# First batch of a sorted-block attention and feed-forward kernel: processed in two block halves, with a hand-written order and the second half under the feed-forward

## Chip, cores and metric

The kernel runs on one core of a Trainium2 chip. The metric is the device time of one execution in microseconds (us). Every time of a kernel below is a median; a figure from a trace is that of the one profiled run. Runs of different calls went to different chips, so kernels of different calls are compared by their ratios to the kernel before.

## The reference, cut to what matters

Attention with a learned block sort, then a bilinear feed-forward. There are 4 batches, 8 heads, 768 rows, head size 64, and 8 blocks of 96 rows.

```python
for _ in range(5):                       # per head, an 8 x 8 matrix
    P = exp(P - max(P)); P = P / sum(P, axis=-1); P = P / sum(P, axis=-2)
k_sorted = einsum('bhij,bhjcd->bhicd', P, k_blocks)   # "mix"; v likewise
scores = q_block @ k_sorted_block.T / 8               # each block on its own
x = softmax(scores) @ v_sorted_block
out = ((x @ w_a) * (x @ w_b)) @ w_out                 # 512 -> 1536 -> 512
```

## The kernel before

A unit of attention is a group: two heads of one batch, 768 rows, four groups to a batch. TensorE transposes q (`q_ps`), mixes k and v with the normalised P (`mix`), makes scores (`sc`) in two tiles of four blocks, transposes v (`vs_ps`), multiplies (`o_ps`), and transposes the result back (`xt_ps`). ScalarE copies k and half of v and does the exp. VectorE copies the rest, takes the reciprocal and scales (`xp`). The first batch goes ahead of everything, and each later batch runs as units between the feed-forward steps of the batch before it:

```python
def C0(g):
    stage_mix(g, "k", ps0, "A", ("act",))
    stage_mix(g, "v", ps0, "A", ("act", "dve"))
def R0(g):
    stage_scores(g, ps0, "A")
    stage_v(g, ps0b, "B")
def O0(g):
    stage_o(g, ps0, "A")
for g in range(1, HP):
    stage_q(g, ps0b, "B")
C0(0); C0(1); R0(0); O0(0); to_xT(0, ps0b, "B")
C0(2); R0(1); O0(1); to_xT(1, ps0b, "B")
C0(3); R0(2); O0(2); to_xT(2, ps0b, "B")
R0(3); O0(3); to_xT(3, ps0b, "B")
# ... then, for each batch b:
steps = [lambda m=m, t=t, b=b: ffn_ab(b, m, t, psF) for m in range(KO) for t in range(2)]
# ... after step s, so many of the next batch's 16 units (mix, scores, o, xT of four groups):
want = -(-(s + 1) * len(units) // (n - 2))
```

TensorE's instructions run in the order written: in the timeline the first mix, whose k and P are there by 14.1 us, starts at 17.68 us, behind the transpose of a q that lands at 17.04 us. GpSimd issues all loads but that of the sort matrix in one stream: the first batch's k, v, q group by group, then w_a and w_b, then the second batch's k, v, q. After those come the spreading of P for the later batches (`s_all`), and w_out.

The softmax here doesn't subtract the row's maximum and nothing guards it: scores larger than these inputs give would overflow.

## Time and profile before

| | before |
|---|---|
| time | 276.93 us (276.44 to 277.31, 3 runs) |
| span of the profiled run | 275.0 us |
| first feed-forward matmul | 44.83 us |
| TensorE busy after 44.83 us | nearly without a gap |

These are lines of the page of the kernel before. The PE and PEclk lines cut the span in 40 slices of 6.9 us; a digit is the busy share in tenths, and PEclk is the granted TensorE clock in tenths.

```profile
span 275.0 us, 5700 instructions
...
PE   0267757999999999999999999999999999999993
...
PEclk9998775999999999999999999999999999999999
```

From the eighth slice on TensorE is full. What can be gained quickly lies in the first seven slices, the "head".

The chain of waits of the kernel before, for one group of the head (start, length, what):

```profile
25.50 1.42 PE mix L145 x24
26.92 0.82 PE sc L166 x16
27.74 0.86 PE vs_ps L177 x8
28.62 0.70 DVE vs_116 L179
29.32 0.04 issue
29.36 0.43 PE o_ps L189 x8
29.81 0.21 DVE rec L193
30.05 0.69 DVE xp L196
30.74 0.13 DVE rec L193
30.89 0.70 DVE xp L196
31.59 0.05 issue
31.63 0.45 PE xt_ps L215 x4
32.08 1.42 PE mix L145 x24
```

One group is a chain through three engines, walked in strict order: mixes, scores, v, VectorE's copy, o, two reciprocal and xp pairs, back-transposes, 6.6 us in all. TensorE holds only part of it. The other part shows among its waits up to 46 us:

```profile
engine line waited for: us in total, times, longest us
...
PE xt_ps L215 <- DVE xp L196: 4.7, 8, 0.8
...
PE q_ps L131 <- DMA q_102<-in_q_dram: 2.4, 1, 2.4
PE o_ps L189 <- DVE vs_115 L179: 1.6, 2, 0.8
```

TensorE waits for xp eight times. The fourth q (q_102) lands late and holds back mixes whose own data are ready. The v copy is waited for twice in the buffer shown and once in each of the two others (0.8 us each).

The windows view of the kernel before (stretch in us, then busy time and instruction count of each engine, then the granted clock):

```profile
core 0: us, PE busy (x) PEld busy (x) DVE busy (x) ACT busy (x) POOL busy (x), PEclk, DMA share, GB/s
...
25.00:28.00 3.00, 3.00 (x48) 2.53 (x49) 0.96 (x2) 1.68 (x4) 1.20 (x3) 0.50 1.32 203
...
38.00:44.83 6.83, 4.12 (x52) 3.22 (x53) 3.80 (x8) 1.50 (x2) 6.81 (x5) 0.54 1.07 164
44.83:48.60 3.77, 3.77 (x30) 2.11 (x31) 0.78 (x2) 0.48 (x1) 3.77 (x7) 0.50 0.83 118
```

The granted clock falls to 0.50 in 25 to 28 us, in 32 to 35 us, and from 38.6 us into the feed-forward, until 48.8 us. Two mixes (24 matmuls) take 1.42 us of the chain at a granted clock of 0.50 here, and 0.67 us later in the span.

### The profile page before, as it was taken

The numbers are of one execution on the slowest core, as the hardware profiler recorded it, in microseconds if no ns is written. First come the engines' busy times: TensorE is split into PE (matmuls) and PEld (weight loads), VectorE is DVE, ScalarE is ACT, GpSimd is POOL, SyncE is SP. The second block draws the span as 40 slices with busy tenths as digits, with TensorE's granted clock in tenths as the row PEclk, the third lists the DMA queues.
The fourth block names the chain that finished last, engine by engine and source line by source line (L and its number), as shares of the span: only waits on it lengthen the run. The fifth ranks groups of instructions, "written<-read, shape, count | busy, mean of one in ns | idle before, by whom it ended". The sixth has DMA issues, their size and how long they took to land.

```text
span 275.0 us, 5700 instructions
## 1 busy us (share of the span) xinstructions
PE 247.8 (90%) x2400; PEld 152.7 (56%) x2408; DVE 130.7 (48%) x284; ACT 98.1 (36%) x194; POOL 48.7 (18%) x67
## 2 busy tenths in 40 slices
PE   0267757999999999999999999999999999999993
PEld 0255544766666545666665546666665456656441
DVE  5835553566565413656564415656654214444211
ACT  2024430535446004463635105354552023333100
POOL 8953489446303000000000000000000000000000
PEclk9998775999999999999999999999999999999999
DMA  7999998999844332000000231000001230000132
GB/s 94 183 202 203 203 200 119 182 201 201 129 74 56 70 114 79 0 4 0 2 2 0 79 114 41 1 2 0 2 4 38 79 114 0 0 2 0 38 117 76
DMA packets 22393, 20.82 MB, mean 76 GB/s; under 512 B 1376, under 2 KB 19296, under 8 KB 22368
## 3 DMA queue, kind: packets, MB, share of 16 engines
q0 software_dynamic: 18864, 14.16, 34.4%
q1 hardware_dynamic: 3504, 6.30, 6.1%
q8 instruction: 19, 0.31, 0.5%
q14 instruction: 6, 0.05, 0.0%
HBM read 28.32 MB, written 6.29 MB: 126 GB/s over the span
## 4 chain that ended last, share of the span: by engine, by line
PE 88%; DVE 4%; DMA 3%; POOL 2%; issue 1%; ACT 0%; DVEq 0%
PE pf L231 46%; PE po L247 22%; PE mix L145 5%; PE vs_ps L177 4%; PE sc L166 3%; PE o_ps L189 3%; DMA q_102<-in_q_dram 3%; PE q_ps L131 2%; PE xt_ps L215 2%; DVE xp L196 2%; DMA p_nat<-in_sort_net_dram 1%; DVE vs_115 L179 1%; DVE rec L193 0%; POOL v_88 L78 0%; POOL q_96 L78 0%
## 5 line engine op out<-in xcount | busy, mean ns | idle before, releaser
L240 DVE TENSOR_TENSOR hT<-a_sb,pf 128x384 bf16<-128x384 bf16 x96 | 53.1, 553 | 66.2 <-PE pf L231 55.1
L231 PE MATMUL pf<-xT,w_a_sb 128*128 128x384 bf16 x384 | 78.9, 328 | 0.6 <-DVE xT L217 0.6
L231 PE MATMUL pf<-xT,w_b_sb 128*128 128x384 bf16 x384 | 78.8, 328 | 0.0
L239 ACT CAST a_sb<-pf 128x384 bf16<-128x384 f32 x96 | 46.0, 479 | 76.8 <-PE pf L231 53.0
L247 PE MATMUL po<-w_out_sb,hT 128*128 128x512 bf16 x280 | 62.9, 379 | 0.3
L231 PEld LDWEIGHTS <-w_b_sb 128*128 128x128 bf16 x384 | 37.8, 98 | 25.3 <-issue 0.7
L231 PEld LDWEIGHTS <-w_a_sb 128*128 128x128 bf16 x384 | 35.1, 98 | 21.8 <-issue 1.1
L247 PEld LDWEIGHTS <-hT 128*128 128x128 bf16 x288 | 27.8, 98 | 32.1
L253 DVE COPY o_sb<-po 128x512 f32<-128x512 f32 x12 | 8.3, 692 | 36.6 <-PE po L247 36.6
L251 ACT COPY o_sb<-po 128x512 f32<-128x512 f32 x12 | 7.0, 585 | 50.2 <-PE po L247 34.9
L196 DVE TENSOR_TENSOR xp<-o_ps,rec 96x512 bf16<-96x512 f32 x32 | 21.2, 684 | 0.5
L215 PE MATMUL xt_ps<-ident,xp 96*128 96x96 bf16 x128 | 9.4, 214 | 4.9 <-DVE xp L196 4.7
L217 DVE COPY xT<-xt_ps 128x768 bf16<-128x768 bf16 x16 | 8.9, 554 | 8.9 <-PE xt_ps L215 8.9
L215 PEld LDWEIGHTS <-xp 96*128 96x128 bf16 x128 | 7.3, 101 | 7.7 <-DVE xp L196 5.9
L155 ACT CAST kT_106<-mix 128x384 bf16<-128x384 f32 x12 | 5.2, 482 | 16.6 <-PE mix L145 16.6
L170 ACT ACTIVATE eT_112<-sc 96x768 bf16<-96x768 f32 x12 | 9.0, 802 | 4.6 <-PE sc L166 4.6
L135 DVE COPY qT<-q_ps 128x768 bf16<-128x768 bf16 x16 | 8.7, 551 | 2.7 <-PE q_ps L131 2.7
L193 DVE RECIPROCAL rec<-o_ps 96x8 f32<-96x8 f32 x32 | 5.2, 185 | 8.9 <-PE o_ps L189 8.9
L170 ACT ACTIVATE eT_114<-sc 96x768 bf16<-96x768 f32 x10 | 7.5, 807 | 0.9 <-PE sc L166 0.9
L170 ACT ACTIVATE eT_113<-sc 96x768 bf16<-96x768 f32 x10 | 7.5, 807 | 0.9 <-PE sc L166 0.9
L131 PE MATMUL q_ps<-ident,q_81 128*64 128x128 bf16 x12 | 0.8, 314 | 7.7 <-DMA q_81<-in_q_dram 7.7
L155 ACT CAST kT_108<-mix 128x384 bf16<-128x384 f32 x10 | 4.3, 482 | 7.6 <-PE mix L145 7.6
(208 smaller groups left out, 204.0 us busy)
## 6 DMA issues: line engine op xcount, KB each, us to landing
out_dram<-o_sb SPq DMA_DIRECT2D x24, 256.0 KB, 2.0
w_a_sb<-in_moe_w_a_dram POOLq DMA_DIRECT2D x4, 384.0 KB, 12.8
w_b_sb<-in_moe_w_b_dram POOLq DMA_DIRECT2D x4, 384.0 KB, 13.4
w_out_sb<-in_moe_w_out_dram POOLq DMA_DIRECT2D x3, 512.0 KB, 8.6
k_77<-in_k_dram POOLq DMA_DIRECT2D x1, 192.0 KB, 3.7
v_79<-in_v_dram POOLq DMA_DIRECT2D x1, 192.0 KB, 4.1
q_81<-in_q_dram POOLq DMA_DIRECT2D x1, 192.0 KB, 4.8
k_86<-in_k_dram POOLq DMA_DIRECT2D x1, 192.0 KB, 4.7
```

Of the source, the lines that this page charges most:

```text
L135: nc.vector.tensor_copy(out=qT.rearrange("p i c t -> p c i t"), in_=q_ps.rearrange("p c (i t) -> p c i t", i=NB))
L145: nc.tensor.matmul(mix[e * D:(e + 1) * D, c // 3, c % 3 * P:(c % 3 + 1) * P], lhsT=src2[:, e, c * D:(c + 1) * D], rhs=s_all[:, 2 * g + e], ...
L155: nc.scalar.copy(out=d1, in_=s1)
L170: nc.scalar.activation(out=eT[:, hf, :, 0:HB], in_=sc[0:BLK, :, 0:HB], func=AF.Exp, scale=float(scale))
L177: nc.tensor.matmul(vs_ps[:, i], lhsT=vT[:, i * BLK:i * BLK + P], rhs=ident, is_transpose=True)
L196: nc.vector.tensor_tensor(out=_ap(xp, hf * NBH * 2 * D, [[NB * 2 * D, BLK], [D, 2], [2 * D, NBH], [1, D]]), in0=_ap(o_ps, 0, [[1024, BLK], ...
L215: nc.tensor.matmul(xt_ps[:, i, :], lhsT=xp[:, i], rhs=ident[0:BLK, 0:BLK], is_transpose=True)
L217: nc.vector.tensor_copy(out=xT[:, g % HP, :].rearrange("p (i t) -> p i t", i=NB), in_=xt_ps)
L231: nc.tensor.matmul(pf[:, 0:HW], lhsT=w_sb[:, kc, m * P:(m + 1) * P], rhs=_ap(xT, kc * S + t * 3 * CG, [[KA * S, P], [CG, 3], [BLK, NB], [1 ...
L239: nc.scalar.copy(out=a_sb, in_=pf[:, 0:HW])
L240: nc.vector.tensor_mul(out=hT[:, m, t * HW:(t + 1) * HW], in0=a_sb, in1=ab[1][:, 0:HW])
L247: nc.tensor.matmul(po, lhsT=hT[:, m, c * P:(c + 1) * P], rhs=w_out_sb[:, m, :], start=(m == 0), stop=(m == KO - 1))
```

## The change

The intent is to start the feed-forward earlier. The first batch is cut into two halves of four blocks. For the first half only half of q is loaded, ahead of k and v. Its four half groups run in a hand-written order on all engines, with 17 dummy matmuls on zeros, meant to keep the clock up, seven of them before P is ready. P itself is copied and spread in two halves. Nine feed-forward matmuls are begun before its last o. The second half becomes units under the first half's feed-forward steps. Weights come in pieces of 256 columns instead of 384. The PSUM pools become one for attention (2 tiles of two banks) and one shared pool of four banks.

```diff
-C0(0); C0(1); R0(0); O0(0); to_xT(0, ps0b, "B")   # ... and so on
+half_mix(0, 0, "k", "act", fill=4)      # fill: dummy matmuls first
+half_mix(0, 0, "v", "dve")
+half_mix(0, 1, "k", "act", fill=1)
+half_scores(0, 0)
+half_v(0, 0)
+half_mix(0, 1, "v", "dve", fill=1)
+half_mix(0, 2, "k", "act", fill=1)
+half_o(0, 0)
+half_scores(0, 1)
+half_v(0, 1)
+half_mix(0, 2, "v", "act", fill=1)
+half_mix(0, 3, "k", "act", fill=1)
+half_x(0, 0, "dve")
+half_o(0, 1)
+# ... same pattern ...
+half_x(0, 2, "act")
+begun = []
+for m, w_sb in ((0, w_a_sb), (0, w_b_sb), (1, w_a_sb)):
+    pf = psF.tile([P, 512], FP32, tag="F", name="pf")
+    ab_mms(pf, w_sb, 0, m, 0, range(KA - 1))
+    begun.append(pf)
+half_o(0, 3)
+half_x(0, 3, "act")
 # ...
+interleave(steps, units_half(), 1)      # 12 steps of the first half, second half as units
+# ... then the other 12 steps and the outputs, with the second batch as units
```

## The prediction

> **What bounds the kernel now.** Two stages. From 46.9 us on, TensorE is the limit: the chain of waits is matmul after matmul until 271.0 us. In the feed-forward an eight-matmul pf group takes 1.30 us, a twelve-matmul po group about 2.6 us; 768 pf and 288 po matmuls make about 187 us. Each of the twelve attention groups between them (768 rows, two heads) costs 3.1 us of TensorE (q 0.46, two mixes 0.67, scores 0.45, v 0.55, o 0.51, back-transpose 0.34). 187 + 37 = 224 us, which is the whole stretch. After it come 0.7 us of VectorE and a 2 us store.
>
> Before it, 44.8 us go to the first batch. The chain there is the normalisation and load issue, the load of the fourth q (landing at 17.04 us, although the normalised weights are ready at 13.5), and four groups in turn, 6.6 us each, in which TensorE waits for VectorE (vs 0.69, reciprocal 0.2 and xp 0.69 twice). In the windows view the granted clock falls to 0.50 at 25 to 28, 32 to 35 and 38.8 to 48.6 us; two mixes take 1.28 us there against 0.67 later. The first feed-forward steps lose about 2 us to it. [...]
>
> **What the change does, with estimates from the durations above.**
> 1. Before the feed-forward only four of eight blocks are done: per group one exp (0.80) instead of two, one reciprocal and xp, half a vs copy. ScalarE and VectorE have about 7 us each for all four groups, overlapped by hand; TensorE has about 7 us plus 2 us of dummy matmuls. Walking through the orders by hand: weights ready and second pc matmuls at 13.5 us, first mix at 14.4, last back-transpose copied at 26.5. The loads needed (half of q, all k and v) land by about 15 us and never bind.
> [...]
> So the feed-forward starts near 27 us, at full clock, against an effective 46.9 us.
> 3. The second half moves under the feed-forward. Mixes do not get cheaper (twelve small matmuls per tile still): about 1.9 us per group, 7.6 us, paid in TensorE time. 1.5 us of pf matmuls were already done inside the head.
> 4. Units come denser: one per step in the second phase of batch 0, against one per 1.75 steps. A back-transpose then follows its o by 1.3 us, while two reciprocal/xp pairs need 1.8 us plus a 0.55 us product in the queue. I allow 3 us of new TensorE stalls there.
>
> Sum: 27 + 187 - 1.5 + 37.2 + 7.6 + 3 + 4 (tail) = 264.3 us span; time exceeds span by 1.9 us: 266 us. Gain about 11 us (4%).
>
> **Signs.** First full-clock pf at 25 to 29 us; clock 1.00 from about 15 us on; second-half mixes about 0.33 us per tile; TensorE 97% busy after the start, with idle before the back-transposes between 47 and 75 us; w_out and later loads landing before use.
>
> **What would make it wrong.** [...] half units costing as much as whole ones (+4); stalls from four shared PSUM buffers in the dense phase (+3); the ScalarE q copies delaying the fifth exp if q lands late (+1 to 2); [...]. The other way: no stalls (-3).
>
> Range 260 to 271.5 us; faster 0.87, within 0.12, slower 0.01.

The sum came to 264.3 us of span, 266 us of time. One of its terms is 0.5 us allowed for the clock, which with the 26.5 us of item 1 makes the 27 us.

## The result

| | before | after |
|---|---|---|
| time | 277.0 us (4 runs) | 267.14 us (266.22 to 267.88, 4 runs) |
| ratio | | 0.9643 (0.9615 to 0.967) |
| span of the profiled run | 275.0 us | 266.1 us |
| feed-forward from (after: last wait of the head over) | 44.83 us | 28.32 us |
| feed-forward of the second batch from | 105.96 us | 97.37 us |

From the second batch on the two spans are the same length: 44.83 to 105.96 and 28.32 to 97.37 us contain the whole difference. The head became 16.5 us shorter, and the first batch's feed-forward 7.9 us longer.

The page after, the lines that answer to those of before:

```profile
span 266.1 us, 6056 instructions
...
PE   0698799999999999999999999999999999999994
...
PEclk9999799999999999999999999999999999999999
```

The waits of TensorE for xp and for xT up to 46 us, after:

```profile
PE xt_ps L224 <- DVE xph L239: 1.4, 2, 1.0
PE pf L323 <- ACT xT L155: 0.8, 2, 0.6
```

The waits for the fourth q and for the v copies are gone from the view. Of the eight waits for xp two are left, in a head that has four half groups and so four xp.

The chain of waits after, for some two microseconds in the middle of the head:

```profile
18.49 0.36 PE o_ps L233 x8
18.85 0.28 PE sc L198 x8
19.12 0.33 PE vs_ps L210 x4
19.45 0.22 PE mixh L161
19.67 0.31 PE mixh L186 x12
19.98 0.32 PE mixh L161
20.30 0.31 PE mixh L186 x12
20.61 0.28 PE xt_ps L224 x4
```

No other engine is on the chain here: TensorE goes from one half group's mix to another's o and scores, and while it does so ScalarE and VectorE work on the rest. "mixh L161" are the dummies. A half group passes in about 2.0 us (its o starts at 18.42, 20.72 and 22.50 us).

The windows view after, for the head from its first mix and the start of the feed-forward (columns as before):

```profile
15.03:23.93 8.90, 8.49 (x183) 5.79 (x183) 5.55 (x14) 5.83 (x10) 6.55 (x9) 1.00 1.42 198
23.93:28.32 4.39, 2.57 (x25) 1.59 (x26) 1.17 (x3) 1.12 (x3) 2.29 (x4) 1.00 1.45 197
...
30.00:33.40 3.40, 3.40 (x53) 1.91 (x48) 0.84 (x3) 1.47 (x5) 2.76 (x3) 0.50 1.39 199
33.40:52.69 19.29, 19.20 (x249) 12.40 (x248) 11.32 (x27) 10.11 (x20) 15.38 (x19) 1.00 1.28 203
```

The last half group has nothing left to overlap with. TensorE is busy only 2.57 of 4.39 us from 23.93 to 28.32 us, and then the granted clock falls to 0.50 from 30.0 to 33.4 us, in the feed-forward. Four pf matmuls take 1.49 us in that stretch and 0.81 us after it. If all of the stretch is bound by TensorE it costs 1.7 us (estimate: half of 3.4).

### The profile page after: what moved, and what is told of

The parts are those of the page before. It is cut to its first block, busy times and chain, and to the rows that moved or that the text cites. A ratio compares the mean times of both kernels' runs of the same rounds, so it can differ in the third digit from the quotient of the medians.

```text
span 266.1 us, 6056 instructions
## 1 busy us (share of the span) xinstructions
PE 250.3 (94%) x2559; PEld 149.9 (56%) x2569; DVE 128.4 (48%) x296; ACT 102.8 (39%) x202; POOL 51.6 (19%) x70
## 3 DMA queue, kind: packets, MB, share of 16 engines
HBM read 28.32 MB, written 6.29 MB: 130 GB/s over the span
## 4 chain that ended last, share of the span: by engine, by line
PE 89%; DVE 7%; ACT 1%; issue 1%; DMA 1%; DVEq 0%
PE pf L323 46%; PE po L351 23%; PE mix L265 3%; PE vs_ps L294 2%; PE o_ps L233 2%; PE q_ps L251 2%; PE sc L283 2%; PE mixh L186 2%; PE xt_ps L308 2%; DVE xp L239 1%; PE mixh L161 1%; DVE hT L344 1%; PE vs_ps L210 1%; DVE xph L239 1%; PE xt_ps L224 1%
## 5 line engine op out<-in xcount | busy, mean ns | idle before, releaser
L343 ACT CAST a_sb<-pf 128x384 bf16<-128x384 f32 x96 | 46.0, 479 | 70.3 <-PE pf L323 48.8
L287 ACT ACTIVATE eT<-sc 96x768 bf16<-96x768 f32 x24 | 18.0, 802 | 4.4 <-PE sc L283 4.4
L239 DVE TENSOR_TENSOR xp<-o_ps,rec 96x512 bf16<-96x512 f32 x24 | 15.7, 683 | 0.2
L92 POOL DMA_DIRECT2D k<-in_k_dram x16 | 11.6, 723 | 20.1 <-PE mix L265 17.7
L155 ACT CAST kT<-mix 128x384 bf16<-128x384 f32 x24 | 10.3, 482 | 10.6 <-PE mix L265 10.6
L92 POOL DMA_DIRECT2D v<-in_v_dram x16 | 11.6, 726 | 3.3 <-PE pf L323 1.5
L233 PEld LDWEIGHTS <-eT 96*128 96x128 bf16 x256 | 10.6, 98 | 2.5
L233 PE MATMUL o_ps<-vs,eT 96*128 96x65 bf16 x256 | 11.4, 193 | 0.0
L296 DVE COPY vs<-vs_ps 96x1024 bf16<-96x1024 bf16 x12 | 8.2, 686 | 4.0 <-PE vs_ps L294 3.9
L92 POOL DMA_DIRECT2D q<-in_q_dram x12 | 8.6, 720 | 3.6 <-DMA w_out_sb<-in_moe_w_out_dram 1.8
L170 PE MATMUL q_ps<-ident,q_first 64*64 64x64 bf16 x96 | 3.1, 223 | 6.2 <-DMA q_first<-in_q_dram 6.2
```

Of the source, the lines that this page charges most:

```text
L92: nc.gpsimd.dma_start(out=to, in_=_ap(t, (b * H + 2 * hp) * S * D, [[W, P], [S * D, 2], [1, W]]))
L155: nc.scalar.copy(out=out, in_=in_)
L233: nc.tensor.matmul(o_ps[:, e, i * (D + 1):(i + 1) * (D + 1)], lhsT=eT[:, hf, e, i * BLK:i * BLK + P], rhs=vs[:, i0 + i, e, 0:D + 1], start ...
L239: nc.vector.tensor_tensor(out=_ap(xp, i0 * 2 * D, [[nxp * 2 * D, BLK], [D, 2], [2 * D, NBH], [1, D]]), in0=_ap(o_ps, 0, [[1024, BLK], [512 ...
L287: nc.scalar.activation(out=eT[:, hf, :, 0:HB], in_=sc[0:BLK, :, 0:HB], func=AF.Exp, scale=float(scale))
L296: nc.vector.tensor_copy(out=vs[:, :, :, 0:D], in_=vs_ps[0:BLK])
```

## Experiments

Twelve kernels ran, all correct. Names starting with `a_` are edits of the changed kernel, `b_` of the kernel before.

My theory was: a group in the head is slow because TensorE waits in order for the other engines. Hand-ordering removes that. The work that moves under the feed-forward is still paid in TensorE time. The rivals were that the move itself is the gain (hidden work is free), that halving is the gain, or that the dummies' clock is the gain.

### Both halves in the head: `a_seq`

```diff
+items = [(h, hp) for h in range(2) for hp in range(HP)]   # eight half groups
+# same order as the change, over eight instead of four
-interleave(steps, units_half(), 1)
+interleave(steps, [], 1)
```

The second half of q is loaded before the weights.

> The changed kernel with both halves of the first batch before the feed-forward, in the same hand-written order (software pipeline over eight half groups instead of four), the second half of q loaded early, no attention of batch 0 under the feed-forward. Theory A (TensorE bound: moved work is still paid, about 7.3 us of matmuls, while it takes about 2.3 us per half group, 9 us, in the head): the feed-forward starts near 37 us and the time is 2 to 4 us longer than the changed kernel, 269 to 271 us. Rival B (the move is the main gain, hidden work is free): 276 us or more.

Measured: 267.68 us, ratio 0.9651 (0.9617 to 0.9685), within noise of the change. The timeline of this run, where its last half group is done and the first begun group goes on, and where the thirteenth step starts (start, length, instruction):

```profile
37.90 0.33 PE L324 MATMUL pf<-xT,w_a_sb 128*128 128x384 bf16 x1
...
52.28 0.81 PE L324 MATMUL pf<-xT,w_a_sb 128*128 128x384 bf16 x4
```

The feed-forward goes on at 37.90 us instead of 28.32, 9.6 us later. Its first 12 steps then take until 52.28 us, 14.4 us; in the change, with the second half as units between them, from 28.32 to 52.69 us, 24.4 us. So the moved half saves 9.6 us in the head and costs 10.0 us under the feed-forward. The two sides aren't pure: the long head carries two dummies for nearly every half group, the change carries the stretch at a clock of 0.50. As the kernels stand, the move is worth nothing: work moved from a head that keeps TensorE busy to a stage that is bound by TensorE was paid either way. The rival is refuted, and my own expectation of 2 to 4 us was too high.

### Halves, but the old order: `a_plain`

```diff
+C(0, 2); C(1, 1); RO(0); half_x(0, 0, "dve")    # C: mixes of k and v; RO: scores, v, o
+C(2, 1); RO(1); half_x(0, 1, "dve")
+C(3, 1); RO(2); half_x(0, 2, "act")
```

The split, the loads, the ten dummies among the mixes and the units under the feed-forward are those of the change.

> The changed kernel with the four half groups of the head in the order of the kernel before (mixes two ahead, then scores, v, o and back-transpose of one group in a row), same dummies and same split. Theory A (hand-ordering is a main part of the gain, since TensorE waits about 2.5 us per half group for vs, exp, reciprocal and xp): head longer by 4 to 6 us, 271 to 273 us. Rival (halving alone did it): within 1.5 us of 267.

Measured: 277.84 us, ratio 1.0018 (0.9993 to 1.0043). Everything was lost, twice what I expected. The waits of TensorE from 12 us on in this run:

```profile
PE xt_ps L224 <- DVE xph L239: 4.1, 4, 1.0
...
PE o_ps L233 <- DVE vs L212: 1.0, 2, 0.5
PE o_ps L233 <- ACT eT L202: 0.6, 1, 0.6
```

and two stretches of its windows view:

```profile
15.00:25.00 10.00, 7.18 (x109) 4.30 (x108) 3.85 (x9) 3.00 (x5) 7.08 (x10) 0.67 1.43 198
25.00:35.00 10.00, 8.01 (x83) 4.89 (x83) 2.46 (x7) 3.00 (x5) 7.07 (x8) 0.56 1.41 198
```

TensorE waits for xp in each half group and for the v copy or the exp in three of them, and the mean clock of every 5 us from 20 to 45 us lies between 0.50 and 0.73. A half group takes 5.2 to 5.5 us (o at 18.53, 23.68, 29.18 us) instead of 2.0. The feed-forward resumes at 36.8 us. Order and clock are not separate here: in the old order the mean clock is 0.67 in 15 to 25 us and 0.56 in 25 to 35 us, against 1.00 from 15.03 to 28.32 us in the change, although the dummies are the same. That the waits are the cause this run alone does not show.

### No dummies: `a_nodummy`

```diff
-for _ in range(n):
+for _ in range(0):
     nc.tensor.matmul(ps[:, 0:cols], lhsT=warm[:, 0:P], rhs=warm[:, 0:cols], ...)
```

> The changed kernel without any dummy matmuls. Their TensorE time in the head (4 before the first mix, 1.8 us) is saved, but if the clock theory holds, mixes and scores of the head run at half clock (granted clock 0.5 somewhere in 15 to 30 us, about 7 us of real matmul time doubles partly): 1 to 4 us slower than 267. If the dummies are only a cost: 1.5 to 2 us faster.

Measured: 266.66 us (265.38 to 268.72), ratio 0.96 (0.9549 to 0.965). Neither expectation came true. The four runs fall into two pairs, 265.4 and 265.5, 267.9 and 268.7; the profile is of the slowest. In it the matmuls of the head do run slower (the eight scores of a half group hold TensorE for 0.43 us instead of 0.28), but the mixes start 2 us earlier (13.06 instead of 15.03 us), and the head ends at 27.90 us, against 28.32. The granted clock is then 0.50 from 28.7 to 35.6 us. In the change the dummies took about as much time as the faster matmuls returned. So the dummies' clock is not what the change's gain rests on: without any dummy the hand-written order keeps the gain, and with the same dummies the old order loses all of it (`a_plain`).

### The kernel before with dummies only: `b_warm`

```diff
+heat = ps0.tile([P, 2, 512], FP32, tag="A", name="heat")
+keep_busy(heat[:, 0], 5)       # before the fourth q
+# three more before each o tile and three before each group's back-transposes
```

> The kernel before, with dummy matmuls alone added in its waits (before the fourth q, before o and before the back-transposes), nothing else. Clock theory as main cause of the gain: granted clock 1.0 up to 50 us and 4 us or more faster, 273 or less. My theory (the wait for VectorE, not the clock, sets the pace of a group; the clock costs about 2 us at the start of the feed-forward and 1 to 2 us in the head): 274 to 275.5 us.

Measured: 272.38 us (272.26 to 272.53), ratio 0.9822 (0.9801 to 0.9842): 5 us, more than I gave the clock. Two stretches of its windows view:

```profile
25.00:35.00 10.00, 8.80 (x146) 5.97 (x147) 5.59 (x12) 5.29 (x10) 3.93 (x6) 1.00 1.31 202
35.00:45.00 10.00, 8.83 (x125) 5.59 (x123) 6.37 (x14) 2.52 (x5) 9.16 (x8) 1.00 1.14 175
```

The clock stays at 1.00 in both, the feed-forward starts at 42.17 us instead of 44.83 and at full speed (its first four pf matmuls take 0.81 us, 1.44 in the kernel before). In the kernel before, the clock was 0.50 in 25 to 28 us, in 32 to 35 us and from 38.6 to 48.8 us. In the old order the dummies stand mostly in waits (TensorE's waits for xp come to 0.8 us instead of 4.7), and, their own time included, they are worth half of what the whole change gained.

### The kernel before without the wait for the fourth q: `b_qlate`

```diff
-for g in range(1, HP):
-    stage_q(g, ps0b, "B")
-C0(0); C0(1); R0(0)
+stage_q(1, ps0b, "B")
+C0(0); C0(1); stage_q(2, ps0b, "B"); stage_q(3, ps0b, "B"); R0(0)
```

> The kernel before with the transposes of the third and fourth q moved behind the mixes of groups 0 and 1 on TensorE, nothing else. In the trace of before TensorE stands 2.4 us for the fourth q (landed at 17.04 us) although the weights of the mixes are ready at about 14 us. Theory: that wait is on the chain, the head gets 2 to 3 us shorter: 274 to 275 us. Rival: the next waits (vs and exp of group 0) eat it: within 0.8 us of 277.

Measured: 275.28 us (273.83 to 276.16), ratio 0.9912 (0.9878 to 0.9947), about 2.4 us. In the profiled run, the fastest of the four, the feed-forward starts at 41.47 us, 3.4 us earlier. This agrees with the theory: the wait was on the chain.

### The end of the head: `a_nobegun`, `a_o3first`, `a_gapfill`

In the change the nine begun matmuls run from 24.1 to 26.0 us, ahead of the last o, whose inputs are ready at 24.2 us. Then TensorE waits 1.0 us for xp and 0.6 us for the copy of xT. Three edits touch that spot:

```diff
# a_nobegun
-for m, w_sb in ((0, w_a_sb), (0, w_b_sb), (1, w_a_sb)):
+for m, w_sb in ():
# a_o3first
 half_x(0, 2, "act")
+half_o(0, 3)
 begun = []
 # ... the nine begun matmuls ...
-half_o(0, 3)
 half_x(0, 3, "act")
# a_gapfill
 half_o(0, 3)
+keep_busy(heat2[:, 0], 5)
 half_x(0, 3, "act")
+keep_busy(heat2[:, 1], 3)
```

> The changed kernel without the nine feed-forward matmuls begun before the last half group's o. In its trace they run from 24.1 to 26.0 us and hold the last o back, whose vs and exp are ready at 24.2 us, by 1.75 us. Theory: begun matmuls buy 1.46 us and cost 1.7 us of delay, so leaving them out changes less than 0.8 us. Rival (they fill idle time): 1.5 us slower.

> The changed kernel with the last half group's o moved in front of the nine begun feed-forward matmuls, so that these fill the wait for its reciprocal and xp. Theory: last o at 24.3 instead of 26.0 us, feed-forward resumes 1.5 us earlier, and with the idle gaps of 1.0 and 0.6 us gone the clock may not fall at 30 us (another 1.5 us): 264 to 266 us. Rival: the wait moves elsewhere: within 0.5 us of 267.

> The changed kernel with dummy matmuls in the two idle gaps before the feed-forward (five between the last o and its back-transpose, three after that). Theory: the fall of the granted clock to 0.50 from 30.0 to 33.4 us comes from these gaps; filled, the clock stays at 1.0 and 1 to 2 us are saved: 265 to 266 us. Rival: the fall has another cause or moves: clock still falls, time within 0.5 us of 267.

| | time | ratio to before (95%) | feed-forward goes on or starts at |
|---|---|---|---|
| the change | 267.14 us | 0.9643 (0.9615 to 0.967) | 28.32 us |
| a_nobegun | 265.06 us | 0.9549 (0.9524 to 0.9573) | 25.93 us, nothing begun |
| a_o3first | 265.06 us | 0.9549 (0.9523 to 0.9576) | 26.77 us, nine matmuls begun |
| a_gapfill | 266.22 us | 0.958 (0.9552 to 0.9607) | 28.46 us |

The windows view of `a_gapfill`:

```profile
25.00:30.00 5.00, 4.69 (x57) 2.50 (x58) 1.56 (x4) 1.18 (x3) 2.48 (x5) 1.00 1.45 197
30.00:35.00 5.00, 5.00 (x90) 3.18 (x90) 2.20 (x6) 3.26 (x7) 4.35 (x5) 1.00 1.37 202
```

With the gaps filled the clock is 1.00 from 30 to 35 us in the profiled run, where the change has 0.50 from 30.0 to 33.4 us, and 0.6% are saved (mean clock of the runs 0.990 to 0.994 in the change, 1.0 in four of five here). Up to the gaps the two profiles are alike (first mix at 15.16 and 15.03 us), so nothing but the filling is seen to differ: the fall in the change came with the gaps. The begun matmuls as placed in the change are a loss. They hold back the last o by 1.75 us, and they come before the wait instead of into it. Leaving them out saves about 1% where I had expected less than 0.8 us. In `a_nobegun`, whose last back-transpose still waits 1.0 us for xp, the clock is 1.00 from 30 to 35 us, too, but its windows view shows a fall earlier, in the head:

```profile
15.00:20.00 5.00, 5.00 (x85) 3.00 (x84) 2.54 (x6) 2.67 (x5) 5.00 (x8) 0.70 1.43 198
```

It is at 0.50 from 14.6 to 18.0 us there, and in `a_o3first` likewise, without making the head longer (third o at 22.55 us, 22.50 in the change, whose four dummies before the first mix took 1.82 us instead of 0.97). Runs of one kernel differ in this (mean clock 0.993 to 1.0 in `a_o3first`), so how much of the 1% is the clock's stays open. Put into the wait they do no more for the time than leaving them out.

### Fewer dummies: `a_lite`, `a_seqlite`

Both put the last o before the begun matmuls and keep the dummies only until the pipeline is full.

```diff
# a_lite, on a_o3first
-half_mix(0, 1, "v", "dve", fill=1)
+half_mix(0, 1, "v", "dve", fill=2)
-half_mix(0, 2, "v", "act", fill=1)      # and the two mixes of half group 3
+half_mix(0, 2, "v", "act")
# a_seqlite, on a_seq
-V(n + 1)
-K(n + 2)
+V(n + 1, 1 if n < 2 else 0)
+K(n + 2, 1 if n < 2 else 0)
```

> The changed kernel with the last o in front of the begun matmuls and dummies only until the third half group's k. Theory: three dummies fewer at 0.21 us each, pace then set by VectorE: 264 to 265.5 us, at most 0.7 us from the run with the last o first. Rival: without them the clock falls in 20 to 30 us: 266 us or more.

> Both halves of the first batch before the feed-forward, as in the earlier run of that kind, but dummies only up to the third half group and the last o in front of the begun feed-forward matmuls. In the earlier run TensorE never waited in the head, 2.7 us per half group of which 0.64 us were dummies. Theory: dummies in a TensorE-bound head are paid in full; eight of them go (about 1.7 us net of new waits) and the order of the last o saves 1 to 1.5 us: 264.5 to 266 us. Rival: TensorE then waits for ScalarE and VectorE instead, clock falls: 267 to 269 us.

Measured: `a_lite` 264.04 us (263.34 to 265.85), ratio 0.9529 (0.9488 to 0.9571), not apart from `a_o3first`. `a_seqlite` 267.37 us, ratio 0.964 (0.9605 to 0.9675), no better than `a_seq`. The time is the one that the rival gave, but its waits for ScalarE and VectorE are not shown. Without the dummies TensorE waits 0.9 and 1.2 us at two places in the late head for which the profile shows no cause, and the mean clock in 35 to 40 us is 0.68. What those two waits are stays open, and with them whether a dummy-free long head could beat the change.

### Whole groups in a hand-written order: `b_hand`, `b_hand2`

If order is the lever, block halves should not be needed. `b_hand` is the kernel before with only its head rewritten:

```diff
-C0(0); C0(1); R0(0); O0(0); to_xT(0, ps0b, "B")   # ... and so on
+K0(0, 3); V0(0)                 # K0, V0: mix of k, of v; 3 dummies; 8 more before P is ready
+stage_q(1, ps0b, "B")
+K0(1)
+R0(0)
+stage_q(2, ps0b, "B")
+V0(1)
+K0(2)
+O0(0)
+R0(1)
+stage_q(3, ps0b, "B")
+V0(2)
+to_xT(0, ps0b, "B")
+# ... same pattern ...
```

> The kernel before with its four whole groups in a hand-written order (mixes of the next groups between scores and o, back-transposes one group late, q transposes spread out), dummies only before the first mix; no block halves, no split q load, nothing of batch 0 under the feed-forward. If ordering alone is the cause of the gain: VectorE has about 3.6 us per group, so the feed-forward starts at 33 to 35 us with full clock, 265 to 268 us, as fast as the change. If the split into halves (finer pieces) is needed: 271 us or more.

Measured: 271.39 us (270.58 to 272.26), ratio 0.9771 (0.9739 to 0.9802). By the number alone this would speak for the halves. The trace says otherwise: the feed-forward starts at 33.09 us, 11.7 us earlier than in the kernel before and with the whole batch done. Then it starves. The start of its feed-forward (timeline), and the two longest waits of TensorE from 12 us on:

```profile
33.09 1.44 PE L239 MATMUL pf<-xT,w_a_sb 128*128 128x384 bf16 x4 [0.65 <-DMA k<-in_k_dram]
...
PE mix L153 <- POOL s_all L269: 3.5, 1, 3.5
PE q_ps L131 <- DMA q<-in_q_dram: 1.4, 1, 1.4
```

The first unit of the second batch comes after one step. Its q lands late, and the spread P (`s_all`) is made on GpSimd only at 39.3 us, behind twelve loads that GpSimd issues first. TensorE stands 1.4 and 3.5 us. The granted clock, at 0.50 already from 30 to 35 us, is 0.50 again from 40 to 45 us. The gain was given back to data that nobody had needed so early.

`b_hand2` moves those needs (three edits at once, so their shares are not known):

```diff
 for c in range(4):
     load_ab(c)
+spread(nc.gpsimd, p_col, 8, 8)          # second batch's P before its loads
 for hp in range(HP):
     load_pair(1, hp)
-for g in range(1, 4):
+for g in range(2, 4):
     spread(nc.gpsimd, p_col, g * 8, 8)
 # units of the second batch seven steps later
-want = -(-(s + 1) * len(units) // (n - 2))
+late = 7 if b == 0 else 0
+want = -(-(s + 1 - late) * len(units) // (n - 2 - late))
 # end of the head: four dummies after the last o, two after its back-transposes
```

> The run with whole groups in a hand-written order reached the feed-forward at 33.1 us, 11.7 us before the kernel before, but TensorE then stood 1.45 us for a q of the second batch and 3.5 us for its mixing weights, with the clock falling to 0.50. Here the same kernel with the second batch's weights spread on GpSimd before its loads are issued, its attention starting seven feed-forward steps later, and six dummies in the last gaps of the head. Theory (the gain was given back to late data of the second batch, block halves are not needed): no TensorE wait over 0.7 us after the start, 263 to 266 us, level with the best form of the change. Rival (other limits follow): 268 us or more.

Measured: 263.68 us (262.98 to 264.27), ratio 0.9486 (0.9459 to 0.9514). The same two views:

```profile
32.66 0.81 PE L239 MATMUL pf<-xT,w_a_sb 128*128 128x384 bf16 x4 [0.31 <-DVE xT L225]
...
PE sc L174 <- DVE vT L165: 1.2, 2, 0.6
PE xt_ps L223 <- DVE xp L204: 0.8, 3, 0.5
```

Both waits lie in the head. The feed-forward starts at 32.66 us with the granted clock at 1.00, and none of TensorE's later waits in this view (up to 100 us) is over 0.2 us. This is faster than the change (0.9643), and its interval overlaps that of its best form, `a_lite`. The block halves, the split load of q, the second half under the feed-forward and the begun matmuls aren't needed for the gain. Whether whole groups in this order need dummies is not tested: `b_hand2` has 17 of them, as many as the change.

## Why the prediction was right

The time was right: 267.1 against 266.0 us, inside the range. Point by point, by the terms of its sum:

- Feed-forward from 27 us: measured 28.3. The first mix was put at 14.4 us and came at 15.0, because the four dummies before it were slow: they took 1.82 us, and 0.97 us in `a_nobegun` and `a_o3first`. The granted clock does not show this. In the change a dummy of 512 columns holds TensorE for 0.54 us on the chain at 15.88 us and for 0.21 us at 17.33 us, both at a granted clock of 1.00. The begun matmuls held back the last o by 1.75 us, which the prediction does not mention: it counts their 1.5 us only as saved.
- "At full clock": wrong. The clock was 0.50 from 30.0 to 33.4 us, about 1.7 us (estimate above). The 0.5 us allowed for the clock (the term above) was too little, and it was looked for at the beginning of the head instead of its end.
- Moved half 7.6 us: its cost was 10.0 us in the change, with the stretch at a clock of 0.50 in it. In `a_o3first`, which has no such stretch, the first 12 steps take from 26.77 to 49.73 us, 23.0 us, or 8.6 us more than the 14.4 of `a_seq`. The term was about 1 us too small.
- New stalls 3 us: too large. In the second phase of the first batch (52.69 to 97.37 us, 44.7 us) TensorE's work is about 43.5 us (estimate: twelve steps at 1.30, six outputs at 2.59, four groups at 3.1), so some 1.1 us. The waits for xp at the back-transposes are there, as forecast, but at most 0.2 us each.
- The errors partly cancel, and that is luck: after its start the prediction had 237.3 us of span left, and 237.8 were measured.

The prediction did not ask which part of the change does it, and its first item reads as if halving were the reason (half the exps, half the copies before the start). That step doesn't survive: halves in the old order gained nothing (`a_plain`), and whole groups in a good order gained more (`b_hand2`). The saving in work before the start was real, and so was the bill for it afterwards (`a_seq`). What pays is that the in-order TensorE finds ready work at each step, so that a group costs its TensorE time instead of its chain (a half group 2.0 us instead of 5.2 to 5.5), and that the gaps at the end of the head are filled (0.6% in `a_gapfill`). The order, with what it does to the clock, was worth about 10.4 us between `a_plain` and the change (estimate: the difference of their ratios, 0.0375, times 277 us); how much of that is the clock's is not shown.

## What to carry to other kernels

When an engine that runs in order, as TensorE does here, leads a chain through others, first interleave the independent chains by hand, before splitting or moving work: the half batch moved under a stage that TensorE bounds saved 9.6 us and cost 10.0 us. After the order is good, look at who needs data earlier than before: the earlier start in `b_hand` stood 1.4 us for a load and 3.5 us for side work on GpSimd. Put filler, useful or dummy, into the wait and not in front of the instruction that starts the wait (ratio 0.9549 in `a_o3first`, 0.9643 in the change), and check the clock after a stage with gaps, not only in it: here the last gap ended at 28.3 us and the clock fell at 30.0 us.
